# An earlier burst of transfers and an earlier phi in a planned two-layer attention and FFN kernel

## The chip, the cores and the metric

The kernel runs on one core of a Trainium2 chip. Its engines are TensorE (PE in the profile; PEld is its weight loading), VectorE (DVE), ScalarE (ACT), GpSimd (POOL) and SyncE (SP). SP computes nothing: it issues nearly all transfers, in the order of its own list, and a transfer at the head of that list that must wait holds up all behind it. The metric is the device time of one execution in microseconds, as the median of the runs shown.

## The reference

The input x has 2048 tokens of 640 features in bf16. The same attention layer A and the same FFN layer B are applied twice, A B A B, each with its own normalisation and a residual:

```python
x = x + A(layernorm(x));  x = x + B(layernorm(x))      # twice
# A: 32 heads of 20 features, 4 segments of 512 tokens
for s in range(4):
    p = softmax(q[s] @ k[s].T * 20**-0.5 + causal_mask)
    a_mem = (phi(q[s]) @ M) / (phi(q[s]) @ z + 1e-6)   # M, z: sums over earlier segments
    o[s] = g * a_mem + (1 - g) * (p @ v[s])            # g = sigmoid(beta), one for each head
    M, z = M + phi(k[s]).T @ v[s], z + sum(phi(k[s]))
y = o @ wo
# phi(t) = t + 1 where t > 0, else exp(t);  B(x) = relu(x @ w1) @ w2, w1 640 x 1728
```

## The kernel before, in words

**Planner.** The kernel function does not write out the order of its instructions. It describes the work as generators ("streams"), and class `Sched` (L190 to L397) runs them against a table of estimated durations and emits one list for each engine. A stream yields an `Op` (an instruction with its possible engines and the events that it waits for), `Need(name)` (go on when the named event has been planned), `Acq(slots)` (take a free buffer) or `Spawn(prio, stream)`. At each step the planner takes the head with the smallest key: its start as estimated, plus a lateness, plus a hand-set value of `SHIFT` for the stream's number and the segment (L355), then priority. `LAND` (L166) holds estimated landing times of the first loads. So a changed estimate, shift or stream moves instructions on all five engines. Whether an `Op` waits on the chip depends on the events given to it; a bare `Need` orders the plan and makes no wait.

**Stages.** For layer a and segment s, `proj_ln` normalises x and has it transposed by DMA (`xnT`; for segments 1 and 2 of the first layer into the still unused `hT`); `proj_one` and `proj_v` make K, Q (feature-major, five chunks of 128 features, into the staging tile `stg`) and V (`v_aug`). K and Q go through DRAM: `spill` (L986) writes a chunk to `scr`, and `fill` (L1030) gathers the heads of two groups, 20 rows at a time, into one of four `pad` tiles with four transfers. `scores`, `exps`, `causal` and `apply` work on one pair of head groups after the other (32 pairs, four for each segment): scores in five rounds of two halves on PE (L1227, 20 rows of the array for each head), the exponentials on ACT (L1289, ten of 1024 columns for each pair), masks on POOL, and the product with V on PE (L1321). Results are transposed by DMA (`otk`) and divided. The memory part is `phi_` (n = 0 for K, 1 for Q), `turn_k` (DMA transpose of phi(K) into `phk`), `mem_write` and `mem_read`. Then come `combine`, the transpose `oT`, `out_proj`, a second normalisation, and `ffn`. PE products are issued at full width (L709) or as four quarters of 32 columns each (L712).

**The start.** `loads` (L555) issues, on SP and ACT, the four tiles of segment 0's x, and on SP wk, wq, wv, the two pairs of tiles of segment 1's x (`x10`, `x11`), and beta. Segment 0 is transposed on PE (L801). `proj_first` (L921) makes K and Q of segment 0 in halves of 256 tokens: all five chunks of K, then of Q, for the first half, then the second half. The first two head groups don't go through DRAM: `first_heads` (L1004) selects their rows with small PE products. Since the w2 tile is not needed early, segment 0's V and segment 1's K and Q are staged in it (`early_w`); the name `w_r` in the profile can thus mean w2 as well as wk, wq, w1.

**Late transfers.** `late_loads` (L574) issues 38 pieces on SP: 4 tiles of segment 2's x, 5 rows of wo, 4 tiles of segment 3's x (13 pieces of 163,840 bytes), 10 halves of w1, and 15 pieces of w2. Each waits for an exponential (L604), so that they spread over the first pairs; w2 also waits until its early guests are done. All wait for `z1`, two memsets of w2's padding.

**phi.** For each chunk (L1066 to L1077): the event `packed`, that is, the chunk's spill has landed (the exp overwrites the staging tile); max(t, 0) + 1 on VectorE into `rtmp` (L1070); exp in place on ACT after the max (L1072); min of both into `phs` on VectorE (L1073), which then frees the staging tile.

Of the kernel before, what the change touches and what calls it, by code (L numbers as in the profile page):

```python
# [7 lines left out]
ALU = mybir.AluOpType  # L8
# [25 lines left out]
PTH = 1280  # L34
BY_TOKEN = (6, G)
FILL = 16
PT_OFF = [0, 512, 1024, 896]


# [120 lines left out]
class Spawn:  # L160
# [2 lines left out]
        self.gen = gen  # L163


LAND = {"x000": 1550.0, "x001": 1600.0, "x010": 1550.0, "x011": 2500.0, "wk": 2900.0, "wq": 2600.0, "wv": 2400.0}  # L166
LONE_NS = 300.0
SWITCH_NS = 96.0
COLS_LAG = 1500.0
# [4 lines left out]
PE_MARGIN = 80.0  # L174
HOLDERS = 1
SHIFT = {
# [9 lines left out]
}  # L186
HOLD_TOL = {"pe": 220.0, "act": 150.0, "dve": 200.0, "pool": 0.0, "sp": 0.0}

# [261 lines left out]
def bass_interleave_layers__memory_aug_infini_attn__dense_activation_relu__prompt_kernel(  # L450
    nc, A_x, A_wq, A_wk, A_wv, A_wo, A_beta, B_x, B_w1, B_w2, out,
):
    with contextlib.ExitStack() as es:
# [101 lines left out]
        def loads():  # L555
            def x_pair(name, t):
                yield from ld("sp", name, 327680, lambda e: e.dma_start(x_sb[:, t:t + 2, :], xs[:, t:t + 2, :]))

            def cols(name, w, src, c0, c1):
                yield from ld("sp", name, 1280 * (c1 - c0), lambda e: e.dma_start(  # L560
                    w[:, :, c0:c1], src.rearrange("(c p) d -> p c d", p=128)[:, :, c0:c1]))

            for t in range(4):
                yield from ld(("sp", "act")[t // 2], "x0%d%d" % divmod(t, 2), 163840, lambda e, t=t: e.dma_start(
                    x_sb[:, t, :], xs[:, t, :]))
            yield from wload("sp", "wk", wk_r, A_wk)
            yield from wload("sp", "wq", wq_r, A_wq)
            yield from wload("sp", "wv", wv_r, A_wv)
            yield from x_pair("x10", 4)
            yield from x_pair("x11", 6)  # L570
            yield from ld("sp", "beta", 16384, lambda e: e.dma_start(
                beta_bc[:], bass.AP(tensor=A_beta.tensor, offset=A_beta.offset, ap=[[0, 128], [1, H]])))

        def late_loads():  # L574

            def x_pieces(s):
                def one(t):
                    return lambda e: e.dma_start(x_sb[:, t, :], xs[:, t, :])
                return [("x%d" % s, 163840, one(4 * s + i)) for i in range(4)]

            def rows(name, w, src, k):
                return (name, 163840, lambda e: e.dma_start(w[:, k, :], src[128 * k:128 * k + 128, :]))

            def half(k, h):
                cs = slice(h * (DFF // 2), (h + 1) * (DFF // 2))
                return ("w1%d" % h, 221184, lambda e: e.dma_start(w1_r[:, k, cs], B_w1[128 * k:128 * k + 128, cs]))

            pieces = x_pieces(2)
            pieces += [rows("wo", wo_r, A_wo, k) for k in range(FC)]
            pieces += x_pieces(3)  # L590
            pieces += [half(k, h) for h in range(2) for k in range(FC)]
            n2 = len(pieces)
            pieces += [rows("w2", w2_r, B_w2, k) for k in range(NFULL)]
            pieces += [("w2", 81920, lambda e, z=z: e.dma_start(
                w2_r[64 * z:64 * z + DREM, NFULL + z, :], B_w2[NFULL * 128:DFF, :])) for z in range(2)]
            z1 = yield Need("z1")
            sems = {}
            left = {}
            for name, _, _ in pieces:
                left[name] = left.get(name, 0) + 1  # L600
            for n, (name, nbytes, fn) in enumerate(pieces):
                if name not in sems:
                    sems[name] = sem_("d_" + name)
                w = yield Need("ex", *divmod(25 + (n - n2) // 2 if n >= n2 else n * 19 // n2, 5))  # L604
                if n == n2:
                    v0 = yield Need("v00")
                    q1 = yield Need("q01")
                    w2w = v0 + q1 + early_done
                tk = yield dma("sp", sems[name], nbytes, fn, w[:1] + (w2w if n >= n2 else []) + z1, issue=540.0, lat=2400.0, rate=345.0)
                left[name] -= 1  # L610
                if left[name] == 0:
                    S.set(name, tks=[tk])
# [306 lines left out]
            return tk  # L919

        def proj_first():  # L921
            order = [(c, n, 0) for n in range(2) for c in range(FC)]
            order += [(c, n, 1) for cs in ((0, 1), (2, 3, 4)) for c in cs for n in range(2)]
            for z, (c, n, h) in enumerate(order):
                if z >= 1:
                    c0, n0, h0 = order[z - 1]
                    yield Need("qkpart", 0, 0, c0, n0, h0)
                tk = yield from proj_part(0, 0, c, n, h)
            xt = yield Need("xts", 0, 0)
            done_with(0, 0, xt[0], tk)  # L930
            done_with(0, 0, xt[0], tk)
# [116 lines left out]
            S.set("filled", a, s, tks=got)  # L1048


        def phi_(n):
            def f(a, s):
                if s == (NSEG - 1, 0)[n]:
# [5 lines left out]
                for c in range(FC):  # L1059
                    if c in (0, 3):  # L1060
                        if n == 0 and (s > 1 or (a, s) == (1, 0)):
                            yield Need("phi", *divmod(NSEG * a + s - 1, NSEG))
                        if n == 1:
                            yield Need("turned", a, s, c // 3)
                        yield Acq([PHS[c // 3]])
                    p = yield Need("packed", a, s, c)  # L1066
                    q = STGS[sx(a, s)][:, c, n, :]
                    dst, dw = phs[:, c * L:(c + 1) * L], PHS[c // 3].tks
                    rt = yield Acq(RT)
                    tr = yield dve(512, 4, lambda e, rt=rt, q=q: e.tensor_scalar(  # L1070
                        rt.ap, q, 0.0, 1.0, ALU.max, ALU.add), p + rt.tks)
                    te = yield act(512, lambda e, q=q: e.activation(q, q, ACT.Exp), [tr] + p, psum=False)  # L1072
                    tp = yield dve(512, 2, lambda e, rt=rt, q=q, dst=dst: e.tensor_tensor(dst, q, rt.ap, ALU.min),  # L1073
                                   [te] + dw)
                    rt.release(tp)
                    done.append(tp)
                    STG[sx(a, s)][n][c].release(tp)  # L1077
                    if sx(a, s):
                        early_done.append(tp)
                    if n == 0:  # L1080
                        if c in (2, 4):
                            S.set("phk", a, s, c // 3, tks=done)
                            done = []
                if n == 1:
                    S.set("phi", a, s, tks=done)
                    if sx(a, s):
                        S.set("q01", tks=done)
            return f

        READ = {}  # L1090
# [580 lines left out]
```

## Time and profile before

| | us |
|---|---|
| median of 3 runs | 558.03 |
| lowest and highest run | 555.7, 560.97 |
| the profiled execution's own time | 554.34 |
| span in its profile | 552.4 |
| PE, ACT, DVE, POOL busy | 541.8, 417.4, 409.6, 194.5 |

The granted TensorE clock is 1.00 in every stretch. A row of instruction groups reads: line, engine, operation, output and inputs with shapes, count, then the busy time and the mean of one in ns, then the engine's idle time just before them and what ended it. In a timeline or chain row, the first number is the start and the second the duration, both in us; on SP it is the issue, not the transfer. A row of DMA issues ends with the median time from issue to landing. A row of waits gives total, count and longest.

### The profile page before, as it was taken

The numbers are of one execution on the slowest core, as the hardware profiler recorded it, in microseconds if no ns is written. First come the engines' busy times: TensorE is split into PE (matmuls) and PEld (weight loads), VectorE is DVE, ScalarE is ACT, GpSimd is POOL, SyncE is SP. The second block draws the span as 40 slices with busy tenths as digits, with TensorE's granted clock in tenths as the row PEclk, the third lists the DMA queues.
The fourth block names the chain that finished last, engine by engine and source line by source line (L and its number), as shares of the span: only waits on it lengthen the run. The fifth ranks groups of instructions, "written<-read, shape, count | busy, mean of one in ns | idle before, by whom it ended". The sixth has DMA issues, their size and how long they took to land.

```text
span 552.4 us, 23437 instructions
## 1 busy us (share of the span) xinstructions
PE 541.8 (98%) x10501; PEld 313.3 (57%) x10501; DVE 409.6 (74%) x1045; ACT 417.4 (76%) x542; POOL 194.5 (35%) x307
## 2 busy tenths in 40 slices
PE   8989799999999999999999999999999999999998
PEld 6644454455664556645556554565466646757756
DVE  4969889788788899887978986668843789737102
ACT  5989689899888887898798878888868787241140
POOL 6336444343444334343433444334412334101000
DMA  8598998564564174546285715647346341432201
GB/s 273 110 209 216 223 210 194 149 151 112 142 123 94 28 124 133 90 73 117 78 190 80 118 23 115 141 93 99 40 103 127 100 69 22 107 58 28 78 2 51
DMA packets 131915, 62.05 MB, mean 112 GB/s; under 512 B 112136, under 2 KB 121864, under 8 KB 131816
## 3 DMA queue, kind: packets, MB, share of 16 engines
q1 hardware_dynamic: 131384, 60.20, 51.7%
q8 instruction: 82, 1.34, 1.1%
q10 hardware_dynamic: 432, 0.37, 0.2%
q14 instruction: 17, 0.14, 0.1%
HBM read 20.57 MB, written 12.85 MB: 60 GB/s over the span
## 4 chain that ended last, share of the span: by engine, by line
PE 87%; DVE 6%; DMA 3%; ACT 3%; issue 0%; SPq 0%; POOL 0%
PE ps L712 48%; PE ps L709 22%; PE ps L1227 8%; PE ps L1321 6%; ACT PT L1289 3%; PE ps L1107 1%; DVE stats L730 1%; DMA otk<-otu 1%; DVE xn_tok L776 1%; PE ps L1164 1%; DMA pad<-scr 1%; PE ps L1501 1%; DMA scr<-stg 1%; DVE w_r L910 1%; DMA scr<-w_r 1%; DMA x_sb<-in_A_x_dram 1%
## 5 line engine op out<-in xcount | busy, mean ns | idle before, releaser
L1289 ACT ACTIVATE PT<-ps 128x1024 bf16<-128x1024 f32 x320 | 308.8, 1030 | 50.5 <-PE ps L1227 49.4
L1301 POOL TENSOR_SCALAR_AFFINE_SELECT PT<-PT 128x512 bf16<-128x512 bf16 x256 | 167.1, 670 | 251.3 <-ACT PT L1289 251.0
L712 PE MATMUL ps<-xnT,w_r 128*32 128x512 bf16 x1868 | 114.1, 380 | 0.0
L1547 DVE TENSOR_TENSOR x_sb<-x_sb,ps 128x320 bf16<-128x320 bf16 (+1 forms) x65 | 31.2, 480 | 57.5 <-PE ps L712 43.9
L712 PEld LDWEIGHTS ps<-xnT,w_r 128*32 128x32 bf16 x1868 | 46.2, 96 | 44.7 <-issue 6.8
L712 PE MATMUL ps<-w_r,hT 128*32 128x320 bf16 (+1 forms) x1912 | 71.3, 296 | 0.0
L1227 PE MATMUL ps<-pad 20*128 20x512 bf16 (+3 forms) x1024 | 63.4, 301 | 3.4 <-DMA pad<-scr 2.0
L709 PE MATMUL ps<-w_r,hT 128*128 128x320 bf16 x367 | 58.4, 300 | 0.0
L730 DVE BATCH_NORM_STATS2 stats<-x_sb 128x6 f32<-128x320 bf16 x124 | 55.6, 473 | 3.0 <-DMA x_sb<-in_A_x_dram 2.3
L712 PEld LDWEIGHTS ps<-w_r,hT 128*32 128x32 bf16 x1912 | 48.5, 97 | 14.6 <-issue 3.2
L1526 ACT ACTIVATE hT<-ps 128x512 bf16<-128x512 f32 x55 | 32.8, 599 | 22.9 <-PE ps L712 22.7
L1227 PEld LDWEIGHTS ps<-pad 20*128 20x128 bf16 x1024 | 17.8, 92 | 52.8 <-ACT PT L1289 24.1
L709 PEld LDWEIGHTS ps<-w_r,hT 128*128 128x128 bf16 x367 | 33.9, 98 | 17.5 <-issue 5.1
L1525 DVE TENSOR_SCALAR hT<-ps 128x512 bf16<-128x512 f32 x49 | 33.6, 688 | 13.5 <-PE ps L712 12.8
L746 POOL TENSOR_TENSOR rstd<-lnU,mhalf 128x2 f32<-128x2 f32 (+2 forms) x26 | 20.8, 801 | 57.7 <-DVE lnU L742 57.1
L1321 PE MATMUL ps<-PT,v_aug 128*21 128x128 bf16 (+3 forms) x896 | 40.2, 299 | 0.0
L712 PE MATMUL ps<-wo_r,oT 128*32 128x320 bf16 x964 | 37.9, 300 | 0.0
L910 DVE CAST stg<-ps 128x512 bf16<-128x512 f32 (+1 forms) x43 | 27.9, 652 | 10.9 <-PE ps L709 5.3
L1443 DVE TENSOR_TENSOR x_sb<-x_sb,ps 128x320 bf16<-128x320 bf16 x64 | 29.5, 478 | 8.4 <-PE ps L712 7.3
L1072 ACT ACTIVATE stg<-stg 128x512 bf16<-128x512 bf16 x50 | 31.8, 640 | 0.8 <-DVE rtmp L1070 0.6
L1415 DVE TENSOR_TENSOR o_sb<-otk,rden 128x320 bf16<-128x320 bf16 x62 | 32.2, 537 | 0.2
L1321 PEld LDWEIGHTS ps<-PT,v_aug 128*21 128x21 bf16 x896 | 22.6, 93 | 17.0 <-issue 0.6
(122 smaller groups left out, 712.1 us busy)
## 6 DMA issues: line engine op xcount, KB each, us to landing
pad<-scr SPq DMA_DIRECT2D x124, 80.0 KB
scr<-stg SPq DMA_DIRECT2D x34, 256.0 KB, 2.7
out_dram<-x_sb SPq DMA_DIRECT2D x15, 160.0 KB, 2.6
w_r<-in_B_w_dram SPq DMA_DIRECT2D x10, 216.0 KB, 2.9
w_r<-in_B_w_dram SPq DMA_DIRECT2D x13, 160.0 KB, 3.0
x_sb<-in_A_x_dram SPq DMA_DIRECT2D x10, 160.0 KB, 3.3
scr<-w_r SPq DMA_DIRECT2D x5, 256.0 KB, 3.0
wk_r<-in_A_wk_dram SPq DMA_DIRECT2D x1, 800.0 KB, 7.0
```

The source lines that it names most:

```text
L709: return e.matmul(view(dst.ap, b), a, b, start=(k == 0), stop=(k == last))
L712: return e.matmul(view(dst.ap[rows], b), part, b, start=(k == 0), stop=(k == last))
L730: tk = yield dve(320, 1, lambda e, c2=c2: e.bn_stats(stats6[:, t, c2, :], x_sb[:, t, c2 * 320:(c2 + 1) * 320]), xt)
L910: te = yield evac(N, 1, lambda e: e.tensor_copy(sg.ap[:, t0:t0 + N], bk.ap[:, 0:N]), lambda e: e.activation(sg.ap[:, t0:t0 + N], bk.ap[:, ...
L1072: te = yield act(512, lambda e, q=q: e.activation(q, q, ACT.Exp), [tr] + p, psum=False)
L1227: fns.append([(lambda e, z=z, j=j, hh=hh, N=N, o=o, sl=sl, q=hh % 2: e.matmul(slot.ap[:, q, o:o + N], sl.ap[32 * hh:32 * hh + DH, z, 0, 12 ...
L1289: tx = yield act(1024, lambda e, dst=dst, src=src: e.activation(dst, src, ACT.Exp, scale=SCALE), sc + pw)
L1301: tm = yield pool(600.0, lambda e, reg=reg: e.affine_select(out=reg, in_=reg, pattern=[[0, 4], [1, 128]], compare_op=ALU.is_ge, fill=0.0, ...
L1321: fns.append((lambda e, OD, j=j, hh=hh: e.matmul(OD.ap[32 * hh:32 * hh + DH + 1, 128 * j:L], VAUG[vx(a, s)][:, j, 4 * g + hh, :], pt.ap[:, ...
L1415: to = yield dve(320, 1, lambda e, z=z, dst=dst: e.tensor_tensor(dst, av[:, z, :, :, 0:DH], rd.ap[:, z].to_broadcast([128, NJ, 4, DH]), AL ...
L1525: th = yield evac(512, 1, lambda e: e.tensor_scalar(hT[:, dc, :], bk.ap[:, :], 0.0, None, ALU.max), lambda e: e.activation(hT[:, dc, :], b ...
L1526: lambda e: e.activation(hT[:, dc, :], bk.ap[:, :], ACT.Relu), [tk] + HT.tks)
```

## The change

It has four parts and a new set of planner constants.

1. **13 late transfers in one go.** The first 13 pieces of `late_loads` wait for nothing and are planned once beta's load is. They stand right behind beta on SP, ahead of the first spill. The waits for `z1` and for the freed guests now stand with the w2 pieces alone.
2. **phi does not wait for the spill.** It starts once the chunk's projection is in the staging tile. The exp writes to `phs` instead of overwriting the staging tile and no longer waits for the max; the min is taken in place in `phs`. A small stream `free_stg` releases the staging tile after spill, max and exp.
3. **x of segment 1 ahead of wv** in `loads`.
4. **First products by chunk:** K for all chunks (first half), then all that is left of chunk 0, then of chunk 1, then the rest.
5. `LAND` and the whole `SHIFT` table hold other values (the table is cut here).

```diff
+AT_ONCE = 13
...
-LAND = {"x000": 1550.0, "x001": 1600.0, "x010": 1550.0, "x011": 2500.0, "wk": 2900.0, "wq": 2600.0, "wv": 2400.0}
+LAND = {"x000": 2170.0, "x001": 2420.0, "x010": 1200.0, "x011": 1450.0, "wk": 3150.0, "wq": 2900.0, "x10": 2750.0, "x11": 2650.0,
+        "wv": 2400.0, "beta": 2400.0}
...
-            yield from wload("sp", "wv", wv_r, A_wv)
             yield from x_pair("x10", 4)
             yield from x_pair("x11", 6)
+            yield from wload("sp", "wv", wv_r, A_wv)
...
-            z1 = yield Need("z1")
...
-                w = yield Need("ex", *divmod(25 + (n - n2) // 2 if n >= n2 else n * 19 // n2, 5))
+                if n < AT_ONCE:
+                    yield Need("beta")
+                    w = []
+                else:
+                    w = yield Need("ex", *divmod(25 + (n - n2) // 2 if n >= n2 else n * 19 // n2, 5))
                 if n == n2:
                     v0 = yield Need("v00")
                     q1 = yield Need("q01")
-                    w2w = v0 + q1 + early_done
-                tk = yield dma("sp", sems[name], nbytes, fn, w[:1] + (w2w if n >= n2 else []) + z1, issue=540.0, lat=2400.0, rate=345.0)
+                    z1 = yield Need("z1")
+                    w2w = v0 + q1 + z1
+                tk = yield dma("sp", sems[name], nbytes, fn, w[:1] + (w2w if n >= n2 else []), issue=540.0, lat=2400.0, rate=345.0)
...
-            order = [(c, n, 0) for n in range(2) for c in range(FC)]
-            order += [(c, n, 1) for cs in ((0, 1), (2, 3, 4)) for c in cs for n in range(2)]
+            order = [(c, 0, 0) for c in range(FC)]
+            order += [(c, n, h) for c in range(2) for n, h in ((1, 0), (0, 1), (1, 1))]
+            order += [(c, 1, 0) for c in range(2, FC)]
+            order += [(c, n, 1) for c in range(2, FC) for n in range(2)]
...
+        def free_stg(a, s, c, n, read):
+            p = yield Need("packed", a, s, c)
+            STG[sx(a, s)][n][c].release(*p, *read)
+            if sx(a, s):
+                early_done.extend(p + read)
+                if len(early_done) == 30:
+                    S.set("q01", tks=early_done)
...
-                    p = yield Need("packed", a, s, c)
+                    p = yield Need("stg", a, s, c, n)
...
-                    te = yield act(512, lambda e, q=q: e.activation(q, q, ACT.Exp), [tr] + p, psum=False)
-                    tp = yield dve(512, 2, lambda e, rt=rt, q=q, dst=dst: e.tensor_tensor(dst, q, rt.ap, ALU.min),
-                                   [te] + dw)
+                    te = yield act(512, lambda e, q=q, dst=dst: e.activation(dst, q, ACT.Exp), p + dw, psum=False)
+                    tp = yield dve(512, 2, lambda e, rt=rt, dst=dst: e.tensor_tensor(dst, dst, rt.ap, ALU.min), [te, tr])
                     rt.release(tp)
                     done.append(tp)
-                    STG[sx(a, s)][n][c].release(tp)
-                    if sx(a, s):
-                        early_done.append(tp)
+                    yield Spawn(4, free_stg(a, s, c, n, [tr, te]))
```

More of the change, by code (lines that the diff above doesn't have):

```diff
@@ L1085, in f @@
                     S.set("phi", a, s, tks=done)
-                    if sx(a, s):
-                        S.set("q01", tks=done)
             return f
```

18 rows, old and new, of the table SHIFT are left out of this document.

## The prediction

> **What bounds the kernel now.** I read the page first (span, busy shares, chain), then the windows by stage, then the waits, and last the timeline of the first 70 us, because the windows leave idle time on TensorE almost nowhere else.
>
> ```profile
> span 552.4 us, 23437 instructions
> PE 541.8 (98%) x10501; PEld 313.3 (57%) x10501; DVE 409.6 (74%) x1045; ACT 417.4 (76%) x542; POOL 194.5 (35%) x307
> PE 87%; DVE 6%; DMA 3%; ACT 3%; issue 0%; SPq 0%; POOL 0%
> ```
>
> TensorE (PE) is busy 541.8 of 552.4 us, and the chain that ends last is 87% PE.
>
> ```profile
> 0.00:10.00 10.00, 7.34 (x71) 5.71 (x72) 5.11 (x14) 5.42 (x12) 4.96 (x18) 1.00 0.81 271
> 0.00:18.70 18.70, 16.04 (x150) 12.59 (x151) 11.06 (x34) 11.77 (x30) 8.78 (x28) 1.00 0.60 203
> 18.70:34.27 15.57, 14.43 (x147) 8.76 (x149) 11.38 (x35) 13.66 (x20) 6.58 (x9) 1.00 0.84 197
> 34.27:62.08 27.81, 25.96 (x381) 12.23 (x382) 25.25 (x63) 27.76 (x31) 15.12 (x23) 1.00 0.99 218
> 62.08:68.77 6.69, 4.69 (x63) 2.88 (x64) 5.22 (x17) 2.55 (x5) 2.33 (x3) 1.00 0.71 187
> 100.00:120.00 20.00, 19.43 (x404) 9.95 (x397) 16.85 (x48) 18.90 (x27) 8.32 (x12) 1.00 0.68 172
> 138.00:448.00 310.00, 310.00 (x6020) 174.44 (x6021) 244.93 (x612) 259.72 (x321) 121.05 (x184) 1.00 0.50 99
> 500.00:552.40 52.40, 50.06 (x1371) 35.37 (x1360) 16.03 (x42) 8.74 (x15) 1.39 (x2) 1.00 0.19 41
> ```
>
> The columns are the stretch, its length, the busy time of PE, weight loads, VectorE (DVE), ScalarE (ACT) and GpSimd, then the granted clock, the DMA share and GB/s. From 138 to 448 us PE has no idle time. All idle time is 552.4 - 541.8 = 10.6 us: 2.66 in the first 10 us, 2.34 at the end, 0.57 at 100:120, and the remaining 5 before 69 us. So the gain has a ceiling near 5.6 us, because nothing in the diff touches the wait for the first tiles, the final store or a matmul's shape. From 34.27 to 62.08 us ACT is busy 27.76 of 27.81: there the exponentials set the pace, not PE.
>
> ```profile
> 34.27 27.75 ACT L1289 ACTIVATE PT<-ps 128x1024 bf16<-128x1024 f32 x30
> ...
> 68.77 1.94 ACT L1289 ACTIVATE PT<-ps 128x1024 bf16<-128x1024 f32 x2 [2.60 <-PE ps L1227]
> ```
> ```profile
> 68.34 0.40 PE L1227 MATMUL ps<-pad 20*128 20x512 bf16 x4 [2.00 <-DMA pad<-scr]
> ```
> ```profile
> 60.08 2.97 DMA scr<-w_r
> ...
> 64.19 4.10 DMA pad<-scr
> ```
>
> I call m0, m1, ... the pairs of head groups in the order of their scores; each has ten exponentials. m1 to m3 run back to back, 30 in 27.75 us. Then m4, the first pair of segment 1, starts only at 68.34, since its spill left at 60.08 and its gathers landed after 68.29. That is the largest stall, 2.00 us of PE. The second:
>
> ```profile
> DVE rtmp L1070 <- DMA scr<-stg: 1.7, 1, 1.7
> PE ps L709 <- DVE w_r L965: 1.1, 1, 1.1
> ```
>
> VectorE stood 1.7 us before phi's max (L1070) because that waits for a spill; two evacuations of V stood behind it, and PE waited 1.1 us for a bank.
>
> **The change part by part.** The due times of the planner are new too, so the order of every engine moves; I take orders and counts from the two compiled programs and durations from the trace.
>
> *PE's work.* Both programs switch into and out of the 20-row score form equally often (40 times before m4). Over the whole program 22 groups of 320 columns go from four quarters to full width, and 19 of 512 the other way.
>
> ```profile
> 48.88 1.24 PE L709 MATMUL ps<-hT,wq_r 128*128 128x512 bf16 x5
> 49.96 0.38 PE L709 MATMUL ps<-hT,wk_r 128*128 128x512 bf16 x1
> ...
> 50.60 1.05 PE L712 MATMUL ps<-hT,wk_r 128*32 128x512 bf16 x16
> ...
> 54.83 0.86 PE L712 MATMUL ps<-wv_r,hT 128*32 128x320 bf16 x20
> ...
> 55.99 0.31 PE L709 MATMUL ps<-wv_r,hT 128*128 128x320 bf16 x1
> ```
> ```profile
> 59.66 1.18 PE L1360 MATMUL ps<-w_r,PT 128*128 128x21 bf16 x40
> ...
> 60.69 0.84 PE L709 MATMUL ps<-wv_r,hT 128*128 128x320 bf16 x5
> ```
>
> One more full-width matmul costs (1.24 - 0.38)/4 = 0.215 us at 512 columns and (0.84 - 0.31)/4 = 0.13 at 320; a group of quarters about (1.05 - 0.38)/3 = 0.22 and (0.86 - 0.31)/4 = 0.14. Total: 22 x -0.01 + 19 x 0.005, so 0, with 0.4 us either way. Work put before m4's first score: 25 more of 512 and 15 more quarter groups of 512, 56 and 9 fewer of 320, and one token-wise apply (1.18) fewer: 5.4 + 3.3 - 7.3 - 1.3 - 1.2 = -1.1 us. Before it was 16.04 + 14.43 + 25.96 + 4.69 - 0.43 = 60.7 us (0.43 lies after 68.34), with 68.34 - 60.7 = 7.65 idle; now 59.6.
>
> *phi off the spill.* The wait of VectorE above goes, and ACT's exp need not follow the max. No instruction is added. Worth up to 1.1 us of PE at 31 us; but the freed VectorE and ACT take four further phi steps ahead of m1 (eight exps against four), and those lie on ACT's path, which is costed next. Releasing the staging tile now needs spill, max and exp; segment 1 has its own staging tile, so the next user is segment 2, long after.
>
> *First products by chunk.* The same twenty half products; the first eight still end as now. ACT from there to m1's first exponential:
>
> ```profile
> L1072 ACT ACTIVATE stg<-stg 128x512 bf16<-128x512 bf16 x50 | 31.8, 640 | 0.8 <-DVE rtmp L1070 0.6
> L911 ACT ACTIVATE stg<-ps 128x512 bf16<-128x512 f32 x22 | 13.2, 600 | 1.2 <-PE ps L712 0.9
> L965 ACT ACTIVATE v_aug<-ps 128x320 bf16<-128x320 f32 x17 | 7.5, 440 | 4.4 <-PE ps L712 3.9 <-PE ps L709 0.4
> ```
> ```profile
> 13.96 0.38 ACT L911 ACTIVATE stg<-ps 128x256 bf16<-128x256 f32 x1 [0.16 <-PE ps L709]
> ```
>
> The eighth evacuation ends at 14.34. The new order puts behind it 8 phi exps (5.12), 5 half evacuations (1.90), the ten exponentials of m0 (in pairs of 1.94, as at 68.77: 9.7), 3 of V (1.32), 7 of 512 columns (4.2): 22.2, so m1 starts no earlier than 36.6. It was 34.27.
>
> *x10 and x11 ahead of wv; 13 transfers behind beta.*
>
> ```profile
> wq_r<-in_A_wq_dram SPq DMA_DIRECT2D x1, 800.0 KB, 8.7
> wv_r<-in_A_wv_dram SPq DMA_DIRECT2D x1, 800.0 KB, 10.4
> ```
> ```profile
> 2.19 0.53 SPq L550 DMA_DIRECT2D wq_r<-in_A_wq_dram  x1
> 2.76 1.01 SPq L550 DMA_DIRECT2D wv_r<-in_A_wv_dram  x1
> 3.81 3.38 SPq L557 DMA_DIRECT2D x_sb<-in_A_x_dram  x2
> 7.24 0.79 SPq L571 DMA_DIRECT2D beta_bc<-in_A_beta_dram  x1
> ...
> 23.63 0.56 SPq L999 DMA_DIRECT2D scr<-stg  x1
> ...
> 27.75 1.61 SPq L1043 DMA_DIRECT2D pad<-scr  x4
> 29.40 1.90 SPq L752 DMA_TRANSPOSE phk<-phs  x1
> ```
> ```profile
> 14.46 0.89 DVE L730 BATCH_NORM_STATS2 stats<-x_sb 128x6 f32<-128x320 bf16 x2
> ```
>
> wq lands at 2.19 + 8.7 = 10.9 and wv at 13.2, so x10 comes 2.3 us sooner; its statistics, now at 14.46, can start at 12.2. wv lands where x11 lands now, near 15; V's first product stands near 17 in the new order, behind eleven half products and the first heads, so that is covered by 2 us and costs 1 for each us beyond. The 13 pieces (163,840 bytes each, 2.13 MB) take SP from 8.03; at the pace of x10 and x11 (3.38 us for four such pieces) that is 11 us, to 19.0. What SP has next, the spill of chunk 1, is ready near 17: 2 us late. Cost 0, because m1's gathers need chunk 2's spill as well. That one left at 23.63; in the new order it stands behind two transposes of segment 1's x and the transpose of phi(K), which waits for VectorE. VectorE's list from 12.2 to that last min has 10 statistics at 0.45, some 20 evacuations, phi steps and normalisations of mostly 0.3 to 0.5, and small ones: about 16 us by this estimate, to 28. Transpose issue 1.9, spill 0.56 of issue and in all 2.97 to landing, four gathers 1.61, the last landing 4.1 after its issue: 28 + 1.9 + 3.0 + 1.2 + 4.1 = 38.2 at the latest, some 2 us sooner with quick landings. ACT says 36.6, so I take 37.5 for m1's first exponential. Ends: 34.3 (as now) and 43 (VectorE's list 5 us longer, a third more than its sum).
>
> Segment 1's first two chunks are spilled before m2, so the 60.08 spill is no longer what m4 waits for; late next is ACT: 37.5 + 27.75 = 65.3, and m4's first score 0.43 sooner, 64.8. PE's idle time before it is 64.8 - 59.6 = 5.2, against 7.65. **Sum:** -2.4 us of stall, +0.4 (the upper end of PE's work, since more products there wait for banks): -2.0. The profiled execution's span 552.4 becomes 550.4, its own time 554.34 becomes 552.3; the median of the runs, 558.03, becomes 556.0. I leave the later 0.57 us and the tail as they are.
>
> **The rivals.**
> *Stalls vanish.* If m1 starts at 34.3, PE sets the pace to m4 and only the first 10 us stay idle: 5 us, with 100:120 5.6. The timed runs lie 3.7 us above the profiled one; DMA share is 0.99 in 34.27:62.08, and ten of the 13 pieces leave it, so run-to-run waits there may go too: 551.5. Against it stands ACT's sum, 36.6.
> *Slower: the transpose of phi(K) on SP.* VectorE is later than 28 with phi's last min, and the transpose, chunk 2's spill behind it and m1's gathers follow. Each us of m1 after 37.5 costs one; from 37.5 + 2.0 = 39.5 the gain is gone. At 43 it is 558.0 + 3.5 = 561.5. For it: VectorE is busy 48.48 of 60 us from 10 to 70 (row below). Against: ACT could start m1 only 1 us sooner anyway.
>
> ```profile
> 10.00:70.00 60.00, 55.00 (x674) 31.45 (x673) 48.48 (x134) 51.55 (x73) 27.85 (x46) 1.00 0.84 194
> ```
>
> *The 13 transfers hold up what follows them.* The two landings above come in the order of issue. If 2.13 MB must be worked off after x10 is there (14.5) at 197 GB/s (18.70:34.27), that ends at 14.5 + 10.8 = 25.3. Segment 1's transposes, issued near 23, then start 2.3 us later, and PE's first use of them, near 29, slips as much: 558.3. At the 271 GB/s of the first 10 us it ends at 22.4 and costs nothing. The Trainium skill (DMA: Bandwidth & Descriptors, Queues, rings and completion order) says that each DMA engine takes descriptors in ring order; the landings agree. The page does not say which of the two rates holds, and that decides.
>
> *New late stalls.* The seven phi exps of segment 1 that are left fall beside m4's exponentials: by the same prices ACT has 14.0 us between the first exponentials of m4 and m5, PE 13.0. If PE loses from 65 to 150 the share that it loses in 34.27:62.08 (1.85 of 27.81), that is 5.7 us: 561.7. For it: ACT's 18.90 of 20 at 100:120. Against: 138:448 has no idle time with ACT at 84%.
>
> The Trainium skill (Perfetto Trace Analysis, Identifying the Most-Contended Engine) holds matmul busy time for a poor measure and weight-load busy time, here 57%, for a good one; by that the ceiling of 5.6 us need not hold. The trace speaks against it here: consecutive matmuls follow each other at the same 0.215 us wherever nothing waits.
>
> **How the numbers follow.** Forecast 0.42 (alone 553.5 to 558.5), stalls vanish 0.26, slower by the transpose 0.12, held up by transfers 0.05, new late stalls 0.15. A measurement here can tell about 1% from no change, 5.6 us. Below 552.4 lies most of the second case, 0.24. Above 563.6 lies a good half of the last case, where it lasts beyond 150 us or meets a late m1, and the far end of the transpose's (m1 past 45): 0.14. The rest is 0.62. The range goes from 549.5 (stalls vanish, with another 2 us of the runs' 3.7) to 562.5.
>
> **What would show it.** Right: no DVE wait on scr<-stg; m1's first exponential at 36.5 to 38.5, m4's near 65; PE idle in 10:70 about 3 us instead of 5. Wrong: m1 after 39.5, PE waiting for pad or hT near 30 to 37, PE idle after 138, or scores of m3 waiting for gathers (chunk 4's spill now stands behind segment 2's transposes).

## The result, and the profile after

| | us |
|---|---|
| changed kernel, median of 8 runs (lowest, highest) | 552.74 (552.52, 552.92) |
| kernel before on the same chip, median of 8 runs (lowest, highest) | 556.58 (555.38, 560.97) |
| ratio, with 95% interval | 0.9923 [0.9898, 0.9948] |
| profiled execution of the changed kernel: own time, span | 552.63, 550.6 |

The changed kernel is 0.8% faster. That is less than the 1% that the prediction thought could be told from no change, but the interval lies clear of 1. Its profiled execution is 1.7 us below that of before; the medians are 3.8 us apart. Both need explaining. First the page after: span, busy shares, and the shares of the chain that ended last.

```profile
span 550.6 us, 23181 instructions
PE 541.7 (98%) x10362; PEld 314.5 (57%) x10363; DVE 419.5 (76%) x1056; ACT 411.3 (75%) x531; POOL 193.3 (35%) x307
PE 85%; ACT 6%; DVE 5%; DMA 1%; POOL 0%; issue 0%
```

PE's work is 541.7 us, against 541.8. So the whole difference is idle time, and the windows tell where it lies (same columns as in the prediction). After:

```profile
0.00:10.00 10.00, 7.08 (x70) 5.21 (x70) 5.53 (x14) 5.21 (x12) 5.25 (x18) 1.00 0.84 281
10.00:70.00 60.00, 57.98 (x685) 31.34 (x686) 52.13 (x137) 56.14 (x79) 27.26 (x47) 1.00 0.93 224
70.00:138.00 68.00, 66.66 (x1145) 37.44 (x1141) 63.37 (x162) 60.77 (x78) 29.19 (x43) 1.00 0.66 139
138.00:448.00 310.00, 309.73 (x6187) 175.80 (x6179) 253.28 (x632) 249.38 (x311) 116.61 (x179) 1.00 0.53 101
500.00:550.60 50.60, 48.30 (x1332) 34.66 (x1324) 15.07 (x40) 8.53 (x15) 1.39 (x2) 1.00 0.19 42
```

Of the kernel before, the one stretch that the prediction did not quote alone:

```profile
70.00:138.00 68.00, 67.43 (x1130) 33.98 (x1129) 58.92 (x149) 63.06 (x84) 27.76 (x42) 1.00 0.71 164
```

PE's idle time went from 2.66 to 2.92 us in the first 10 us, from 5.00 to 2.02 in 10:70, from 0.57 to 1.34 in 70:138, from 0 to 0.27 in 138:448, and stays at 2.3 at the end. With 0.1 us less work that is 0.26 - 2.98 + 0.77 + 0.27 - 0.04 - 0.1 = -1.8 us, the difference of the spans. The gain is where it was looked for, and a third of it is given back later. Four waits of PE for VectorE between 90 and 96 us, of 0.22 to 0.33 us, make 1.04 us of the 1.34 in 70:138.

The two large stalls are gone. PE's timeline after, around the first score of m1, the longest stall left between 11 and 70 us, and the first score of m4 (a row without a bracket did not wait):

```profile
36.41 0.39 PE L1238 MATMUL ps<-pad 20*128 20x512 bf16 x4
...
45.41 0.72 PE L1332 MATMUL ps<-PT,w_r 128*21 128x512 bf16 x16 [0.45 <-DVE w_r L916]
...
64.47 0.39 PE L1238 MATMUL ps<-pad 20*128 20x512 bf16 x4
```

Windows up to m1's first score, and from there to m4's (same columns). In the first PE has the least idle time, in the second ACT:

```profile
10.00:36.41 26.41, 25.43 (x256) 16.42 (x259) 24.53 (x76) 23.13 (x42) 11.07 (x21) 1.00 0.78 209
36.41:64.47 28.06, 27.03 (x356) 11.75 (x354) 23.64 (x52) 27.48 (x31) 14.15 (x22) 1.00 1.06 233
```

ACT's timeline after. Its exponentials of m1 start at 36.84; the phi exps L1088 now write to `phs`:

```profile
32.30 0.63 ACT L1088 ACTIVATE phs<-w_r 128x512 bf16<-128x512 bf16 x1
...
36.84 1.94 ACT L1300 ACTIVATE PT<-ps 128x1024 bf16<-128x1024 f32 x2 [0.40 <-PE ps L1238]
```

SP's list after (start, time of the issue):

```profile
2.76 1.08 SPq L559 DMA_DIRECT2D x_sb<-in_A_x_dram  x2
3.88 0.47 SPq L552 DMA_DIRECT2D wv_r<-in_A_wv_dram  x1
4.40 2.16 SPq L573 DMA_DIRECT2D beta_bc<-in_A_beta_dram  x1
...
6.60 2.34 SPq L580 DMA_DIRECT2D x_sb<-in_A_x_dram  x4
8.98 2.33 SPq L584 DMA_DIRECT2D wo_r<-in_A_wo_dram  x5
11.35 2.25 SPq L580 DMA_DIRECT2D x_sb<-in_A_x_dram  x4
17.45 0.33 SPq L1007 DMA_DIRECT2D scr<-stg  x1
...
27.83 1.44 SPq L758 DMA_TRANSPOSE phk<-phs  x1
...
32.08 3.34 SPq L1051 DMA_DIRECT2D pad<-scr  x8
...
36.75 1.32 SPq L758 DMA_TRANSPOSE otk<-otu  x1
...
42.66 0.93 SPq L1007 DMA_DIRECT2D scr<-w_r  x2
...
46.96 2.29 SPq L1051 DMA_DIRECT2D pad<-scr  x6
```

The 13 pieces are issued from 6.60 to 13.60. Segment 1's first spills leave at 42.66 (before: 53.81), m3's gathers at 46.96, and nothing of the 13 pieces stands between them. The exp at 32.30 reads a chunk of segment 1 (staged in `w_r`) that is spilled at 42.66 at the earliest: with the old wait for the spill this order could not exist.

### The profile page after: what moved, and what is told of

Its sections match the earlier page's. It is cut to its first block, busy times and chain, and to the rows that moved or that the text cites. A ratio compares the mean times of both kernels' runs of the same rounds, so it can differ in the third digit from the quotient of the medians.

```text
span 550.6 us, 23181 instructions
## 1 busy us (share of the span) xinstructions
PE 541.7 (98%) x10362; PEld 314.5 (57%) x10363; DVE 419.5 (76%) x1056; ACT 411.3 (75%) x531; POOL 193.3 (35%) x307
## 4 chain that ended last, share of the span: by engine, by line
PE 85%; ACT 6%; DVE 5%; DMA 1%; POOL 0%; issue 0%
PE ps L718 48%; PE ps L715 21%; PE ps L1238 8%; PE ps L1332 5%; ACT PT L1300 5%; PE ps L1118 1%; DVE xn_tok L782 1%; DMA otk<-otu 1%; DVE stats L736 1%; PE ps L1512 1%; PE ps L1175 1%; ACT phs L1088 1%; DMA x_sb<-in_A_x_dram 1%; DVE om_sb L1133 0%; POOL rstd L752 0%; DVE x_sb L1454 0%
## 5 line engine op out<-in xcount | busy, mean ns | idle before, releaser
L718 PE MATMUL ps<-xnT,w_r 128*32 128x512 bf16 x1804 | 108.9, 380 | 0.2 <-DVE rden L1421 0.2
L718 PE MATMUL ps<-w_r,hT 128*32 128x320 bf16 (+1 forms) x2000 | 74.0, 296 | 0.0
L718 PEld LDWEIGHTS ps<-w_r,hT 128*32 128x32 bf16 x2000 | 52.1, 97 | 13.8 <-issue 1.9
L715 PE MATMUL ps<-w_r,hT 128*128 128x320 bf16 x345 | 54.3, 300 | 0.0
L1536 DVE TENSOR_SCALAR hT<-ps 128x512 bf16<-128x512 f32 x56 | 38.3, 685 | 10.5 <-PE ps L718 8.3
L715 PEld LDWEIGHTS ps<-w_r,hT 128*128 128x128 bf16 x345 | 32.0, 98 | 16.5 <-issue 4.9
L1537 ACT ACTIVATE hT<-ps 128x512 bf16<-128x512 f32 x48 | 28.4, 600 | 16.7 <-PE ps L718 16.2
L916 DVE CAST stg<-ps 128x512 bf16<-128x512 f32 (+1 forms) x49 | 31.4, 642 | 9.9 <-PE ps L718 5.3
L782 DVE TENSOR_SCALAR xn_tok<-x_sb,mv,rstd 128x640 bf16<-128x640 bf16 x60 | 31.0, 554 | 2.3 <-POOL rstd L752 2.0
L1089 DVE TENSOR_TENSOR phs<-phs,rtmp 128x512 bf16<-128x512 bf16 x60 | 28.5, 475 | 5.4 <-ACT phs L1088 5.1
```

What stands on the lines that cost most here:

```text
L715: return e.matmul(view(dst.ap, b), a, b, start=(k == 0), stop=(k == last))
L718: return e.matmul(view(dst.ap[rows], b), part, b, start=(k == 0), stop=(k == last))
L782: nm = lambda e, bx, t, k: e.tensor_scalar(bx.ap[:, k * D:k * D + D], x_sb[:, t + k, :], mv[:, t + k, 0:1], rstd[:, t + k:t + k + 1], ALU. ...
L916: te = yield evac(N, 1, lambda e: e.tensor_copy(sg.ap[:, t0:t0 + N], bk.ap[:, 0:N]), lambda e: e.activation(sg.ap[:, t0:t0 + N], bk.ap[:, ...
L1536: th = yield evac(512, 1, lambda e: e.tensor_scalar(hT[:, dc, :], bk.ap[:, :], 0.0, None, ALU.max), lambda e: e.activation(hT[:, dc, :], b ...
```

## The experiments

The first four kernels and the last were made from the kernel before with its planner's order left as it is, so that only the part named differs. The others were made from the changed kernel.

**The kernel before, once more.** No edit.

> The kernel before, unchanged, profiled once more. Its timed runs lie 1.0 to 6.6 us above its first profiled execution (554.34). If waits for transfers between 30 and 70 us make the difference, a profile of a longer execution has more than the 5.0 us of idle TensorE time in 10:70 that the first one has, at the waits for gathers, transposes or spills, and the rest of the span is as before. If it is something else (clock, tail), the extra time stands elsewhere.

Measured: 555.11 us (553.68 to 557.29), ratio to before 0.9999 [0.9979, 1.0020]. So the comparison can tell about 0.2%. The profiled execution took 554.45 us, no longer than the first one, so it can't say where longer executions spend their extra time.

**phi off the spill, alone.** Order of the kernel before; only the waits and the exp's place change:

```diff
-  te = act: activation(q, q, Exp)        waits: tr, spill
-  tp = dve: tensor_tensor(dst, q, rt)    waits: te, dst free
+  te = act: activation(dst, q, Exp)      waits: chunk staged, dst free
+  tp = dve: tensor_tensor(dst, dst, rt)  waits: te, tr
```

> The kernel before with every engine's list in the same order; only phi is changed: it waits for its chunk in the staging tile and not for the spill, and the exp writes to phs. Theory (the new order brings the gain, by letting segment 1's spill leave before pair m2): the wait of VectorE on scr<-stg (1.7 us) and the TensorE stall of 1.1 us at 31 go, m1 starts up to 1.2 us sooner, but the spill near 60 us still starts m4, so 0.3 to 1.2 us in all. Rival (the wait for the spill itself was what cost): 2 us or more.

Measured: 558.08 us (555.74 to 561.10), ratio 1.0048 [1.0027, 1.0068]: slower. The profiled execution is the longest of them (561.10), so its stalls may be larger than the usual ones. Seven of its 11 executions show a mean granted clock of 0.997; the other four have a median of 557.0 us, against 555.0 for the kernel before at full clock on the same chip. In PE's timeline of this run the stall of 1.14 us near 31 is gone, and PE reaches m1's gathers before they have landed. Two more stalls stand later:

```profile
32.83 0.40 PE L1234 MATMUL ps<-pad 20*128 20x512 bf16 x4 [1.27 <-DMA pad<-scr]
...
70.14 0.40 PE L1234 MATMUL ps<-pad 20*128 20x512 bf16 x4 [2.45 <-DMA pad<-scr]
...
85.95 0.39 PE L1234 MATMUL ps<-pad 20*128 20x512 bf16 x4 [1.97 <-ACT PT L1296]
```

The last is a new wait that the edit itself brings. `phs` holds the phi(K) that a DMA transposes into `phk`; the exp now writes `phs`, so it must wait until that transpose has read it. Formerly only the min, the last of the three steps, touched `phs`. ACT's timeline of this run, and ACT's waits:

```profile
83.44 0.63 ACT L1079 ACTIVATE phs<-w_r 128x512 bf16<-128x512 bf16 x1 [2.56 <-DMA phk<-phs]
```
```profile
ACT phs L1079 <- DMA phk<-phs: 3.9, 2, 2.6
```

**13 transfers in one go, alone.** Order of the kernel before, the first 13 pieces taken out of SP's list and put behind beta. The waits that stood ahead of them stay where they were in the list, and SP still meets them.

```diff
-  SP: beta, spill, x2, x2, hT, spill, x2, ... pad, x2, wo ... pad, wo, x3 ...
+  SP: beta, x2 x4, wo x5, x3 x4, spill, hT, spill, ...
```

> The kernel before with every list in the same order, but the 13 transfers stand behind beta on SP; their old waits stay where they were. Theory: 0.2 to 1.0 us, from gathers and transposes that land sooner between 34 and 62 us (DMA share there 0.99, falls to about 0.75); m4 still waits for the spill near 60. Rival (transfers in the full stretch cause both the stalls and the spread of the runs): the median falls by 2 us or more, and the runs lie within 1 us of each other.

Measured: 554.98 us (553.91 to 557.13), ratio 0.9992 [0.9977, 1.0007]: nothing. The DMA share of 34.27:62.08 falls from 0.99 to 0.76, about as expected, but m4's first score still waits 1.68 us for its gathers. The runs spread over 3.2 us, so the rival by which these transfers alone cause the spread falls.

**Three parts, old order.** Both edits above and wv behind x10 and x11 on SP.

> The kernel before with the same order on TensorE, VectorE, ScalarE and GpSimd, and three parts of the change: phi without the wait for the spill, 13 transfers behind beta, x of segment 1 ahead of wv. Theory: 0.8 to 2 us faster, m4's first score still at 66 to 68 us, well above the 552.7 of the changed kernel. Rival (the parts as such bring the gain, not the new order): within 0.5 us of 552.7.

Measured: 556.04 us (555.17 to 558.46), ratio 1.0017 [1.0003, 1.0032]. Its waits hold the same two things as with phi alone, in a smaller size:

```profile
ACT phs L1095 <- DMA phk<-phs: 2.0, 1, 2.0
PE ps L1250 <- DMA pad<-scr: 1.8, 2, 1.1
```

So these three parts do not bring the gain in the old order. What is left for it is the fourth part (first products by chunk) and the order that the planner makes of all four.

**The changed kernel, once more.** No edit; a yardstick for the next runs.

> The changed kernel once more, unaltered, on the chip that runs the next three, so that they have a yardstick of their own. Both theories: 552.5 to 553.0, ratio to before about 0.993 to 0.996, its runs within 0.5 us of each other.

Measured: 552.81 us (552.30 to 554.51), ratio 0.9953 [0.9936, 0.9969], span 550.6. The runs spread over 2.2 us and not over 0.5 as expected. Losses below are counted from this 552.81. The runs with only wo late, wv ahead of x, otk first and exp off `phs` were taken on another chip, without the unaltered changed kernel beside them; the nearest to it there is the run with otk first, 552.59.

**The changed code with the old tables.** `LAND` and `SHIFT` of the kernel before.

```diff
-LAND, SHIFT of the change
+LAND, SHIFT of the kernel before
```

> The changed code with the planner's old tables (LAND and SHIFT of before), so the planner writes another order for the same parts. Theory 'the order': the parts bring nothing without the tuned order, 555 to 558, with waits for pad or for an exp behind the transpose of phi(K). Rival 'the parts': any order that knows of them keeps the gain, 552.3 to 553.5.

Measured: 616.27 us (613.67 to 618.74), ratio 1.1089 [1.1053, 1.1125]; span 614.5 and PE busy 92% of it. This is worse than either theory had it. The old shifts belong to another plan. The run shows only that the parts with an order not tuned for them can lose 11%, not what a good order without one of them would do.

**Nine of the 13 pieces late.** The changed order, only SP's list edited:

```diff
-  beta, x2 x4, wo x5, x3 x4, spill, ... pad x8, phk, otk, hT x2, spill ...
+  beta, x2 x4, spill, ... pad x8, wo x2, phk, otk, wo x3, hT x2, x3 x4, spill ...
```

> The changed kernel in its own order, but nine of the thirteen pieces (the five of wo, the four of x of segment 3) go back behind the gathers of m1 and m2 and the transposes that follow, where the kernel before had them; nothing else moves. Theory 'SP's room': nine issues of 0.45 to 0.75 us put 4 to 6.5 us ahead of the spills and gathers of m3 and m4; m3's gathers leave at 51 to 53 instead of 46.96 and land near 56, past m3's first score at 55.33: PE waits up to 2.3 us for pad there, time 553.3 to 555, and the runs spread over 1 us. Rival 'the burst is idle': SP has slack, within 0.4 us of the changed kernel.

Measured: 563.48 us (563.15 to 563.86), ratio 1.0140 [1.0116, 1.0164]: 10.7 us lost, more than expected and for another reason. VectorE's timeline of this run (the statistics L747 of segment 3's x) and PE's behind it:

```profile
40.29 0.69 DVE L927 CAST w_r<-ps 128x512 bf16<-128x512 f32 x1
50.27 0.49 DVE L747 BATCH_NORM_STATS2 stats<-x_sb 128x6 f32<-128x320 bf16 x1 [9.29 <-DMA x_sb<-in_A_x_dram]
```
```profile
51.62 2.31 PE L726 MATMUL ps<-hT,wq_r 128*128 128x512 bf16 x5 [8.72 <-DVE w_r L927]
```

The new order has these statistics in VectorE's list at 40 us, so x of segment 3 must be there by then. The evacuations stand behind them, and PE behind those. The burst is not a matter of SP's room alone: VectorE's order relies on it.

**Only wo late.** The five pieces of wo as in the run above, x of segment 3 back in the burst.

```diff
-  beta, x2 x4, wo x5, x3 x4, spill, ... pad x8, phk, otk, hT x2 ...
+  beta, x2 x4, x3 x4, spill, ... pad x8, wo x2, phk, otk, wo x3, hT x2 ...
```

> The changed kernel in its own order, but only the five pieces of wo are moved back, to the places that they had in the run with nine late; x of segment 3 stays in the burst. It splits that run's 10.7 us. If the landing of x of segment 3, for which VectorE's statistics stood 9.29 us, is the whole of it: 552.5 to 553.3. If the room on SP is a part of it (five issues, some 3.4 us, ahead of the spills and gathers of m3 and m4): 554 or more, with PE waiting for pad.

Measured: 554.91 us (554.54 to 555.69), 2.1 us over the changed kernel. SP's room does count, though not through m3's gathers, as had been expected: PE's largest waits are for VectorE (1.15 us at 43.74, 0.74 at 46.87 and 0.88 at 59.58, where the changed kernel has 0.21, 0.45 and none), and VectorE stands for transposes that leave SP later. Its waits on `otk`, whole run (in the changed kernel the first is 3.9 us in all and the second 0.4):

```profile
DVE rden L1429 <- DMA otk<-otu: 5.5, 4, 1.7
...
DVE otu L1353 <- DMA otk<-otu: 1.8, 1, 1.8
```

**Short exponentials.** The changed order with exps of phi cut to 16 columns:

```diff
-  activation(dst, q, Exp)
+  activation(dst[:, :16], q[:, :16], Exp)
```

> The changed kernel, but the eight phi exponentials that ACT does ahead of m1 (five of segment 0's phi(K), three of segment 1's) cover 16 columns instead of 512, so phi of those chunks is not computed rightly; every instruction stays in its place. They fall from 0.63 to some 0.2 us, 3.4 us in all. Theory of the prediction 'ACT's sum sets m1, and m1 sets m4': m1's first exponential near 33.5 instead of 36.8, m4's near 62, time 549.5 to 551. Rival 'PE's own list sets m1': m1's first exponential at 36.3 or later, time 552.2 to 552.9.

Measured: 552.55 us (552.20 to 554.76), within 0.3 us of the changed kernel. Only the five exps of segment 0 became short ahead of m1 (the three of segment 1 there belong to K, and those of Q were cut), so ACT had 5 x 0.42 = 2.1 us less to do, not 3.4. ACT's timeline of this run:

```profile
30.75 0.21 ACT L1089 ACTIVATE phs<-stg 128x16 bf16<-128x16 bf16 x1
32.01 0.60 ACT L917 ACTIVATE w_r<-ps 128x512 bf16<-128x512 f32 x1 [1.05 <-PE ps L715]
...
32.84 0.62 ACT L1089 ACTIVATE phs<-w_r 128x512 bf16<-128x512 bf16 x1
...
37.45 1.94 ACT L1301 ACTIVATE PT<-ps 128x1024 bf16<-128x1024 f32 x2 [0.40 <-PE ps L1239]
```

m1 starts at 37.45, no earlier than the 36.84 of the changed kernel. (The 0.6 us more come from the start: in this execution PE waited 1.06 us for wk, up to 9.83, and its list stands 0.61 us later at 30.74 as at m1's first score.) The time that ACT saved became waits for PE, 1.05 us of it at 32.01. So ACT's sum does not set m1 in the new order. ACT's waits for PE, and PE's 25.43 us of work in the 26.41 from 10 us to m1 in the changed kernel, speak for PE's own list, which no run shortened.

**wv ahead of x again.** The changed order with wv back ahead of x10 and x11 on SP.

```diff
-  wk, wq, x10, x11, wv, beta
+  wk, wq, wv, x10, x11, beta
```

> The changed kernel in its own order, but wv goes back ahead of x10 and x11 in SP's list; nothing else moves. Theory of the prediction 'x10 2.3 us sooner': undone, VectorE's statistics of x10 and the normalisations, transposes and products behind them come 2 us later, PE waits near 28 to 30 us, 553.8 to 555.2. Rival 'covered': something else holds that chain, or VectorE has other work meanwhile, 552.5 to 553.2.

Measured: 553.53 us (553.12 to 554.53), 0.7 us lost (0.9 against the run with otk first, on the same chip); neither expectation had the size or the place. In VectorE's timeline the first statistics of x10 end their wait at 14.80, and a stall of PE stands at 17.68, in segment 0's products:

```profile
14.80 0.89 DVE L742 BATCH_NORM_STATS2 stats<-x_sb 128x6 f32<-128x320 bf16 x2 [1.32 <-DMA x_sb<-in_A_x_dram]
...
16.96 0.67 DVE L1035 CAST pad<-ps 128x512 bf16<-128x512 f32 x1
```
```profile
17.68 0.72 PE L721 MATMUL ps<-xnT,wq_r 128*128 128x256 bf16 x5 [1.45 <-DVE pad L1035]
```

VectorE stood for x10, its evacuation of the first heads came late behind that, and PE waited 1.45 us for the bank. In this execution nothing of it was made good: PE's products that stand at 59.68 in the changed kernel stand at 61.21, and the span is 1.6 us longer. At 554.22 us it is one of the longer ones; the median lost half as much.

**The transpose of otk first.** PE's only stall above 0.4 us between 11 and 500 us is the 0.45 us at 45.41; VectorE stood 0.78 us for the transpose that SP issues at 36.75. An attempt at a faster version:

```diff
-  SP: pad x8, phk, otk, hT x2
+  SP: pad x8, otk, phk, hT x2
```

> The changed kernel in its own order, but the transpose of otk that leaves SP at 36.75 us goes ahead of the transpose of phi(K) at 35.47; an attempt at a version faster than both. In the changed kernel VectorE stood 0.78 us for that transpose at 41.62, and PE 0.45 us at 45.41 behind it. Theory 'the stall is the late landing': it lands 0.8 us sooner, the gap at 45.41 goes, 552.1 to 552.5. Rival: the transpose of phi(K), now 2 us later, becomes the one waited for, or PE's gap stays for another reason, 552.6 to 553.5.

Measured: 552.59 us (552.20 to 554.25), ratio 0.9949 [0.9927, 0.9971], against 0.9953 [0.9936, 0.9969]: no difference that can be told. VectorE no longer waits for that transpose, and PE's stall is still there:

```profile
45.47 0.72 PE L1338 MATMUL ps<-PT,w_r 128*21 128x512 bf16 x16 [0.55 <-DVE w_r L922]
```

So that stall is VectorE's own list, not the transpose.

**phi alone, exp off `phs`.** The run with phi alone, but with the two targets exchanged, so that VectorE's max meets the wait for the transpose and ACT's exp does not:

```diff
-  tr = dve -> rt      te = act -> dst (waits: dst free)
+  tr = dve -> dst (waits: dst free)      te = act -> rt
```

> The kernel before in its old order with phi off the spill, as in the run with phi only, except that ACT's exp writes the small ring of scratch tiles and VectorE's max writes phs, so the wait for the transpose of the former phi(K) moves from ACT's exp to VectorE's max. Theory: the run with phi only lost its 2.7 us to that wait on ACT (3.9 us, twice, with PE idle 1.97 us at 85.95 behind one); without it 555 to 556.3, no ACT wait on phk<-phs, unless VectorE's max now stands as long and PE with it. Rival: the loss is the late spill and the gathers of m4 (2.45 us at 70.14): 557 to 559 as before.

Measured: 567.04 us (564.65 to 568.96), ratio 1.0209 [1.0179, 1.0238], far slower. The wait left ACT and grew on VectorE, where every evacuation stands behind it. VectorE's waits over the run, and PE's largest stall:

```profile
DVE phs L1077 <- DMA phk<-phs: 12.5, 4, 4.2
```
```profile
83.17 0.58 PE L715 MATMUL ps<-wo_r,oT 128*128 128x320 bf16 x3 [3.47 <-DVE x_sb L1450]
```

The wait on `phs` is real and follows whichever step first writes it. In the old order the cheapest of the three places is the last step, where the kernel before had it. How much of the 2.7 us of phi alone it explains is not settled by this, since the stall for m4's gathers (2.45 us, against 2.00 in the kernel before) has a part too. A scratch tile of its own for the exp, which would remove the wait from both, was not tried.

## Why the prediction was right, and where it was not

**The stalls (right).** m4's first score was put at 64.8 and came at 64.47; m1's first exponential was put at 37.5 and came at 36.84; PE's idle time in 10:70 was put near 3 and is 2.02. PE's work ahead of m4's first score was put at 59.6 us and is 59.53, its idle time there at 5.2 and is 4.94. VectorE's wait on scr<-stg is gone, PE waits for no gathers before m4. From m1 to m4 ACT sets the pace as forecast: 28.06 us between the first scores, where 27.75 was taken.

**ACT's sum sets m1 (wrong, with the right number).** The forecast let ACT start m1 "no earlier than 36.6" because of its work. With 2.1 us of that work away, m1 came no earlier. What the runs speak for is PE's own list, which is busy 25.43 of 26.41 us up to m1; that is read from the trace and from one run, and not tested by a shorter list. A sum of one engine's work that comes out at the measured time is not yet its cause.

**"I leave the later 0.57 us as they are" (wrong by 1 us).** In 70:138 the idle time grew by 0.77 us and in 138:448 by 0.27. The rival of new late stalls had the direction and not the size (5.7), and it had PE waiting for ACT, where the four waits of 70:138 are for VectorE. The allowance of +0.4 us for PE's work was not needed (-0.1). So the span, put at 550.4 and measured at 550.6, is in part luck: -2.7 us ahead of m4 (forecast -2.4), +1.0 later (0), -0.1 of work (+0.4).

**phi (a wait overlooked).** The forecast took the edit as a wait removed. It also adds one: the exp writes `phs` and so waits for the transpose. In the new order it costs nothing, for no ACT wait on phk<-phs is among the changed kernel's waits; in the old order it cost 3.9 us on ACT, and the part alone lost 0.48%. The rival that the transpose of phi(K) on SP is late did not come about: it left SP at 27.83, where 28 was forecast.

**The 13 transfers (pace wrong, cost right, use underrated).** They were to take SP until 19.0; they ended at 13.60, and the spill behind them left at 17.45 with time to spare. They hold up nothing, as forecast. But the forecast gave them no worth beyond that, and the new order rests on them: nine put back cost 10.7 us, five 2.1 us.

**x ahead of wv (a landing read where none was waited for).** Forecast: x10 2.3 us sooner, so its statistics at 12.2 instead of 14.46, with no price of its own in the sum. But the statistics at 14.46 had no wait for x; they stood behind VectorE's own memsets. In the run of three parts they start at 14.38 with x ahead, in the changed kernel at 13.41, both again without a wait for x. In the new order the place of wv counts: undone it costs 0.7 us, through VectorE and the first heads.

**The step from the profile to the median (wrong by 3.3 us).** The forecast set the median 3.7 us above the profiled execution, as for the runs shown before. The changed kernel's first eight runs lie at 552.52 to 552.92, around its profiled 552.63, so the median came to 552.74 instead of 556.0. Most of the 3.7 us was the draw of three runs: over 85 later executions the median of the kernel before is 555.51, 1.2 us above its profile. Under the forecast's rival of vanishing stalls a smaller spread was named as a possibility, put down to transfers. The run with the 13 transfers alone kept a spread, so they alone are not the cause. What goes with a part of the spread is the granted clock (below).

**The ceiling.** The gain kept under the ceiling of 5.6 us that PE's idle time sets. Weight loads rose from 313.3 to 314.5 us while the time fell, so they were no better a measure here than busy matmuls.

## What to carry to other kernels

A part that removes a wait can gain nothing when the order stays as it is: PE just arrives earlier at the next thing that is late. Such a part should be judged with the order that is planned for it, and an order should be read for what it takes for granted (here x of segment 3 at 40 us). When a step gets a new destination, look for who still reads that tile: the wait moves to the first step that writes it, and in the old order here it cost least on the last.

## What the runs showed of the hardware

**The granted clock can fall after a stall and add to its cost.** Windows of the run with nine pieces late, where PE stopped at 42.90 and went on at 51.62 (the clock is the third number from the right):

```profile
44.00:46.00 2.00, 0.00 (x0) 0.00 (x0) 0.00 (x0) 1.03 (x2) 1.13 (x2) 1.00 1.29 212
46.00:48.00 2.00, 0.00 (x0) 0.00 (x0) 0.00 (x0) 0.00 (x0) 0.00 (x0) 0.51 1.12 293
...
54.00:56.00 2.00, 2.00 (x29) 0.89 (x32) 1.22 (x3) 1.22 (x2) 0.00 (x0) 0.50 0.88 211
56.00:58.00 2.00, 2.00 (x25) 0.86 (x18) 1.58 (x3) 1.64 (x2) 1.21 (x2) 0.93 0.62 180
```

The clock halves some 3.1 us into the stall and comes back some 5 us after work resumes; the five matmuls at 51.62 take 2.31 us, where five such took 1.24 in the kernel before. The stall, 8.5 us longer than the 0.21 us that the changed kernel has at this place, and 4.7 us of work at half the clock (2.3 us by estimate) together make about the 10.7 us that this run lost. Windows of the run with phi alone show the same after a stall of only 1.97 us, at 85.95, and no such thing after the one of 2.45 us at 70.14:

```profile
70.00:72.00 2.00, 1.86 (x13) 1.00 (x14) 0.89 (x2) 1.43 (x2) 0.00 (x0) 1.00 1.25 138
...
86.00:88.00 2.00, 2.00 (x9) 0.76 (x10) 0.00 (x0) 2.00 (x3) 1.19 (x2) 0.61 1.34 125
88.00:90.00 2.00, 2.00 (x7) 0.69 (x5) 1.50 (x6) 0.32 (x1) 0.84 (x2) 0.54 0.45 99
```

The Trainium skill (TensorE: Matmul & The Clock Gate, Part 1: The HAM clock gate) says that the clock is halved after one idle window of about 3.4 us, and that the window runs freely. The first run's 3.1 us is near that; the second shows a fall after 1.97 us of idle time, so stalls shorter than the window can bring it too. Nor does the length of the stall alone decide. In the run with exp off `phs` the clock stays at 1.00 through the stall of 3.47 us that ends at 83.17, and falls behind one of 2.17 us that ends at 292.94:

```profile
82.00:84.00 2.00, 0.83 (x11) 0.33 (x11) 1.58 (x5) 0.00 (x0) 0.00 (x0) 1.00 0.67 134
...
294.00:296.00 2.00, 2.00 (x9) 0.91 (x6) 1.97 (x7) 0.00 (x0) 0.00 (x0) 0.50 0.66 124
```

Over three sets of runs, 31 of 85 executions of the kernel before show a mean granted clock of 0.994 to 0.997; their median is 556.87 us, that of the other 54 is 554.61. Of 19 executions of the changed kernel none is below 1.000, and their medians are 552.74 and 552.81. So at full clock the two kernels are 1.8 us apart, the same as their spans, whose difference is stall. Over all 85 the median of the kernel before is 555.51, another 0.9 us, which goes with the falls. The eight runs of the first table (556.58) lie 1.1 us above that; their clocks are not on record. The clock does not explain all of the spread: the 54 at full clock still lie from 553.72 to 556.66. That the stalls of 1 to 2 us at 31 and 68 us bring these falls in the kernel before is argued from the runs above and not shown; its own profiled execution shows none, and the run with wv ahead of x, with a stall of 1.45 us, shows none in 12.

**SP's time for the same issues differs between executions.** The 13 pieces of 163,840 bytes took 7.0 us to issue, 0.54 each, where the forecast took the 3.38 us of x10 and x11 as the price of four such pieces. But x10 and x11, behind the same wk and wq, took 1.08 us in the changed kernel's profile and 1.16 in its second, and 3.18, 3.08 and 2.72 us in the runs with short exponentials, with only wo late and with otk first, whose lists are the same up to there. So one profile's time for such an issue is not yet its price; what makes it vary is not shown.

**What stays open.** The part "first products by chunk" was not tried alone, nor the kernel before with the new tables, so how much of the gain is the new order by itself is not known. phi with the old wait cannot be tried in the new order, as the exp at 32.30 precedes its spill.
